# Opening and convolution of an adaLN + S4 + gMLP block: a tick plan replaced by a written list of single steps, phases rounded on TensorE, and K's 32-point product in quarter tiles

## The chip, the core and the metric

One core of a Trainium2 chip. The metric is the device time in microseconds (us) of one execution of the whole program. TensorE appears in the profile as PE (matmuls) and PEld (weight loads), VectorE as DVE, ScalarE as ACT, GpSimd as POOL and SyncE as SP. SP and POOL issue most of the DMAs.

## The reference

The block has two halves with a modulation `mod = silu(c) @ w_mod` in front. The first half is a state-space layer (S4) over 2048 tokens and 576 channels with 128 states each:

```
h  = layernorm(x) * (1 + ca) + sa
K  = real(einsum("dn,dnl,dn->dl", C, exp(dt*A*l), dt*B))     # 576 x 2048
y  = irfft(rfft(h, 4096) * rfft(K, 4096))[:2048] + h * Dskip
x1 = x + ga * y
```

The second half is a gated MLP (`gelu(h2 @ w_in)`, a 2048 x 2048 spatial product, `w_out`) on `x1`. All is float32 at the interface. The change touches only the first half.

## The kernel before

`ssm` (L165) computes the first half. It has two parts, here called opening and convolution.

**Opening.** `poles` (L199) turns the raw S4 parameters into phases and log magnitudes, split in three bf16 parts and stored to DRAM (`pa_d`, `pb_d`); generator `p0` does channel quarter 0, `p1` quarters 1 to 3, at three times the width. `poles_load` (L296) brings them back as `lb`, `lc`, `la`. `mod_unit` (L342) makes six modulation rows. `ln_stats`, `ln_rows` and `ln_half` (L389 to L434) normalise x and do the first forward stage of the transform of h, stored to `u1_d`.

**K, in 36 groups of 16 channels.** `e_unit` (L442): a product into PSUM and `Exp` on ACT. `t_unit` (L456): phases in turns into a PSUM pair `pa`, reduced to the nearest whole turn. For the first `NR = 10` groups TensorE does the rounding by adding and subtracting 12582912 inside the accumulation (L469 beside the L465 products), and DVE copies the rest out (L477). For the other 26 groups ACT adds the constant (L480) and DVE subtracts (L481). L482 takes the absolute value, and `s_unit` (L485) does two `Sin`. `p_unit` (L490): four DVE products. `kg_unit` (L504): 32 products of 128x32 by 128x64 into one bank, copied out by ACT (L514). `d_unit` (L516): a DVE addition of Dskip to 4 columns. `k1_unit` (L520): K's 32-point product, eight float32 products of the 128x64 `kk[:, i]` with a 128x128 block-diagonal matrix that holds the same 32-point block four times, copied out by DVE for odd groups from 11 on (L533), by ACT otherwise (L535).

**Convolution, in 36 units of 512 columns** (five channel blocks of 128, 128, 128, 128 and 64): `u_unit` (L574) a forward product; `z_unit` (L584) K's last stage and the pointwise product on DVE (L591); `v_unit` (L594) the inverse product, stored to `v_d`; `y_unit` (L637), 20 of them, the last stage and the residual addition, stored to `x1_d`. A channel block can be convolved when its eight groups of K are done; it needs `u1_d` of all tokens.

**What sets the order.** The opening, with groups 0 to 8, is a string of units (L725). After it come ticks 9 to 39 (L735): each tick runs one group's units at fixed lags in one of three rotations, and the convolution units by a plan (L656). Then a written tail (L768 to L823) mixes the last units with the preparation of the MLP's first weights. In the ticks the engines' streams are left to the framework; `mlp.tied` marks instructions that keep program order. PSUM tiles: `ps2()` gives one of 2 pairs of banks (`ps`), `ps1()` one of 4 single banks (`pk`). Line 152 (`Pin`) is the recorded line of every tied instruction, so those groups are told apart by their tiles.

After `ssm`, `phase_a` and `phase_b` do the MLP; they are unchanged.

Of the kernel before, what the change touches and what calls it, by code (L numbers as in the profile page):

```python
# [9 lines left out]
F32 = mybir.dt.float32  # L10
# [8 lines left out]
D = 576  # L19
NST = 128  # L20
L = 2048
# [7 lines left out]
GRP = 16  # L29

# [89 lines left out]
def body(tc, I, out):  # L120
    nc = tc.nc
    V, A, G, T, S = nc.vector, nc.scalar, nc.gpsimd, nc.tensor, nc.sync
    with ExitStack() as ctx:
# [6 lines left out]
        V.memset(consts_s[:, 0:1], MAGIC)  # L130
# [34 lines left out]
def ssm(tc, I, x1_d, consts_s, dram, mod_d, mlp):  # L165
    nc = tc.nc
    V, A, G, T, S = nc.vector, nc.scalar, nc.gpsimd, nc.tensor, nc.sync
    magic, halfpi, one = consts_s[:, 0:1], consts_s[:, 1:2], consts_s[:, 2:3]
    HC = 288
    CW = 16 * 9 * 128  # L170
    with ExitStack() as ctx:
# [17 lines left out]
        small = cp.tile([128, 6, 128], F32, name="small")  # L189
        r1 = [small[:, 0], small[:, 1]]  # L190
        fwd, inva, invb, ones = (small[:, i] for i in range(2, 6))
# [7 lines left out]
        def poles(c0, c1, Q, own=None):  # L199
# [8 lines left out]
            def split3(*items):  # L208
# [8 lines left out]
                for src, dst, k, pt, q in parts:  # L217
                    A.activation(pt[:, 0], src, AF.Copy)
                    V.tensor_tensor(q, src, pt[:, 0], op=ALU.subtract)
                    A.activation(pt[:, 1], q, AF.Copy)  # L220
                for src, dst, k, pt, q in parts:
                    V.tensor_tensor(pt[:, 2], q, pt[:, 1], op=ALU.subtract)
                    for c in range(c0, c1):
# [9 lines left out]
            def run():  # L233
# [3 lines left out]
                A.activation(dt, ldt, AF.Exp)  # L237
                V.tensor_tensor(tau, dt, tau, op=ALU.mult)
# [8 lines left out]
                V.tensor_tensor(q1, Ci, Bi, op=ALU.mult)  # L247
                V.tensor_tensor(wr, wr, q1, op=ALU.subtract)
# [7 lines left out]
                V.tensor_tensor(mn, ax, ay, op=ALU.min)  # L256
                V.tensor_scalar(mx, mx, 1e-37, None, op0=ALU.max)
                V.reciprocal(rnd, mx)
                V.tensor_tensor(mn, mn, rnd, op=ALU.mult)
                yield  # L260
                A.activation(lw, mx, AF.Ln)
                AP = mlp.tied.scalar
                AP.activation(q1, mn, AF.Square)
                AP.activation(q1, q1, AF.Ln, bias=one)
                AP.activation(ph, mn, AF.Arctan)
# [4 lines left out]
                split3((al, pb_d, 0), (tau, pa_d, 0))  # L270
                yield
                V.scalar_tensor_tensor(lw, q1, 0.5, lw, op0=ALU.mult, op1=ALU.add)
                V.tensor_tensor(lw, lw, ldt, op=ALU.add)
                split3((tau64, pa_d, 3), (lw, pb_d, 3))
                yield
                V.tensor_scalar(ph, ph, 1.0 / (2 * math.pi), None, op0=ALU.mult)
                V.tensor_tensor(ax, ay, ax, op=ALU.is_gt)
                V.tensor_scalar(ay, ph, -2.0, 0.25, op0=ALU.mult, op1=ALU.add)
                V.tensor_tensor(ay, ay, ax, op=ALU.mult)
                V.tensor_tensor(ph, ph, ay, op=ALU.add)  # L280
                V.tensor_scalar(ay, ph, -2.0, 0.5, op0=ALU.mult, op1=ALU.add)
                V.scalar_tensor_tensor(ay, wr, 0.0, ay, op0=ALU.is_lt, op1=ALU.mult)
                V.tensor_tensor(ph, ph, ay, op=ALU.add)
                yield
                V.scalar_tensor_tensor(ay, wi, 0.0, ph, op0=ALU.is_lt, op1=ALU.mult)
                V.scalar_tensor_tensor(ph, ay, -2.0, ph, op0=ALU.mult, op1=ALU.add)
# [1911 lines left out]
```

## Time and profile before

| | |
|---|---|
| median of 3 runs | 1754.17 us (1753.26 to 1754.69) |
| profiled execution, first to last instruction (span) | 1749.5 us |
| instructions | 36390 |
| busy: PE, PEld, DVE, ACT, POOL | 1654.4, 1241.1, 1256.1, 834.3, 250.5 us |
| first 512-column product of phase A (`pz<-wz,nt`) | 424.2 us |

The span leaves out what lies before the first and after the last instruction; the profiled execution has no separate whole time, so the median less the span, 4.7 us, stands for that. `ssm` fills the first 424 us. In the views "busy" is the union of the instructions' spans. For pipelined matmuls the distance from one start to the next says more than the length of one.

### The profile page before, as it was taken

The page shows a single profiled execution, that of the slowest core. Times are in us where ns is not written, and L with a number is a line of the kernel's source. Part 1 is how long each engine was busy: PE and PEld are TensorE (multiplying, and loading weights), DVE is VectorE, ACT ScalarE, POOL GpSimd, SP SyncE. Part 2 cuts the span into 40 slices and gives each one's busy share as a digit, 9 for nine tenths or more (in the row PEclk, how much of TensorE's full clock was granted, in tenths as well). Part 3 has the DMA queues.
Part 4 walks back from the last instruction along what each step waited for, and adds up shares of the span by engine and source line. Part 5 has one row for each costly group of instructions (what it writes and reads, how often), then busy time and mean ns, then how long its engine had stood idle before and what let it go on. Part 6 is the DMA issues. An engine that isn't in the chain of part 4 may idle for free.

```text
span 1749.5 us, 36390 instructions
## 1 busy us (share of the span) xinstructions
PE 1654.4 (95%) x15174; PEld 1241.1 (71%) x15174; DVE 1256.1 (72%) x2259; ACT 834.3 (48%) x1121; POOL 250.5 (14%) x412
## 2 busy tenths in 40 slices
PE   2788999996999999999999999999999999999999
PEld 1344666664455446777878888888888888888887
DVE  7876999948999997888898767797444387334432
ACT  6877999834677665445443433343221233122210
POOL 4421332342122110000000000000111100111100
PEclk9897999998999999999999999999999999999999
DMA  8477656798698798777656887764766563556531
GB/s 227 136 223 229 187 155 170 207 271 248 215 292 272 222 249 290 258 253 261 221 193 205 289 290 263 241 231 138 246 219 231 195 224 106 194 197 208 193 110 41
DMA packets 182934, 376.24 MB, mean 215 GB/s; under 512 B 39105, under 2 KB 102977, under 8 KB 182001
## 3 DMA queue, kind: packets, MB, share of 16 engines
q1 hardware_dynamic: 138304, 168.50, 31.9%
q0 software_dynamic: 37984, 178.55, 31.2%
q10 hardware_dynamic: 6480, 26.86, 3.8%
q8 instruction: 119, 1.95, 0.5%
q14 instruction: 47, 0.38, 0.1%
HBM read 263.11 MB, written 101.31 MB: 208 GB/s over the span
## 4 chain that ended last, share of the span: by engine, by line
PE 32%; issue 28%; DVE 18%; DMA 4%; POOL 3%; ACT 2%; SPq 0%; POOLq 0%; ACTq 0%; DVEq 0%
PE ps L152 28%; POOL zset L1906 2%; DMA zset<-set_d 2%; DVE bsz L152 2%; DVE zset L152 1%; DVE n L152 1%; DVE gt L152 1%; DVE rq L152 1%; DVE wsp L152 1%; PE pk L578 1%; PE pk L598 1%; PE pk L590 1%; DVE pg L499 1%; DVE wso L152 1%; DVE ft L481 1%
## 5 line engine op out<-in xcount | busy, mean ns | idle before, releaser
L152 PEld LDWEIGHTS <-zset 128*128 128x128 f16 x7182 | 701.9, 98 | 92.6 <-DVE zset L152 7.6
L152 PE MATMUL ps<-wsp,zset 128*128 128x256 f16 x6048 | 667.7, 273 | 7.2 <-DVE zset L152 5.8
L152 PE MATMUL pz<-wz,nt 128*128 128x512 f16 (+1 forms) x1120 | 221.9, 358 | 9.0 <-DVE nt L152 4.3
L152 ACT ACTIVATE z<-gt 128x1024 f16<-128x1024 f32 x56 | 59.0, 1054 | 287.0 <-DVE gt L152 287.0
L152 PEld LDWEIGHTS <-nt 128*128 128x128 f16 x1120 | 109.1, 98 | 115.7 <-DVE nt L152 5.8
L1906 POOL DMA_DIRECT2D zset<-set_d x96 | 50.8, 529 | 869.1 <-PE ps L152 619.7
L152 DVE SCALAR_TENSOR_TENSOR gt<-ps,sc,bsp 128x512 f32<-128x512 f32 x36 | 27.0, 750 | 205.5 <-PE ps L152 203.8
L152 PE MATMUL ps<-wout,z 128*128 128x288 f16 x1344 | 170.0, 286 | 0.0
L152 PEld LDWEIGHTS <-z 128*128 128x128 f16 x1344 | 131.5, 98 | 33.0
L152 PE MATMUL ps<-n2o,zset 128*128 128x256 f16 x1134 | 128.2, 273 | 0.0
L152 DVE SCALAR_TENSOR_TENSOR gt<-ps,sc,gt 128x512 f32<-128x512 f32 (+1 forms) x180 | 122.2, 696 | 7.6
L152 DVE TENSOR_TENSOR raw<-raw 128x512 f32<-128x512 f32 (+2 forms) x228 | 119.2, 528 | 11.2 <-DMA raw<-z_d 6.9
L152 ACT ACTIVATE zset<-raw 128x1792 f16<-128x1792 f32 x48 | 81.2, 1691 | 58.3 <-PE ps L152 25.3
L152 DVE TENSOR_TENSOR zset<-raw,zset 128x1792 f16<-128x1792 f32 x48 | 97.0, 2020 | 15.9 <-ACT zset L152 15.9
L152 DVE TENSOR_TENSOR z<-ps,z 128x512 f32<-128x512 f32 (+1 forms) x126 | 72.0, 599 | 36.8 <-ACT z L152 26.7
L152 ACT ACTIVATE wsp<-raw,sc 128x1792 f16<-128x1792 f32 x25 | 44.6, 1785 | 42.7 <-DVE raw L152 35.0
L152 ACT ACTIVATE z<-z,sc 128x1024 f32<-128x1024 f32 x21 | 24.1, 1148 | 75.6 <-DVE z L152 71.9
L152 ACT ACTIVATE z<-pz,sc 128x512 f32<-128x512 f32 (+1 forms) x96 | 52.0, 582 | 16.2 <-DMA z_d<-z 9.8
L152 PE MATMUL ps<-n2q,wf 128*128 128x512 f16 x252 | 55.7, 379 | 0.0
L152 ACT ACTIVATE z<-z,nm,r 128x1152 f32<-128x1152 f32 x24 | 31.5, 1342 | 49.7 <-DVE nm L152 29.3
L152 PE MATMUL ps<-wout,z1b 128*128 128x288 f16 x384 | 52.6, 286 | 0.5 <-ACT z1b L152 0.5
L152 DVE SCALAR_TENSOR_TENSOR wsp<-raw,sc,wsp 128x1792 f16<-128x1792 f32 x25 | 51.9, 2078 | 0.0
(345 smaller groups left out, 2452.7 us busy)
## 6 DMA issues: line engine op xcount, KB each, us to landing
zset<-set_d POOLq DMA_DIRECT2D x96, 896.0 KB, 4.9
raw<-z_d SPq DMA_DIRECT2D x48, 512.0 KB, 5.5
set_d<-zset ACTq DMA_DIRECT2D x24, 896.0 KB, 5.9
z_d<-z POOLq DMA_DIRECT2D x32, 576.0 KB, 9.7
zset<-wa_d POOLq DMA_DIRECT2D x18, 896.0 KB, 4.9
raw<-in_w_spT SPq DMA_DIRECT2D x25, 512.0 KB, 4.4
set_d<-zset SPq DMA_DIRECT2D x12, 896.0 KB, 5.5
u_d<-st1o POOLq DMA_DIRECT2D x16, 576.0 KB, 4.8
```

What stands on the lines that cost most here:

```text
L152: return self.tc.keep_in_program_order(f(*a, **k))
L481: V.scalar_tensor_tensor(f, f, MAGIC, pa, op0=ALU.subtract, op1=ALU.subtract)
L499: V.tensor_tensor(pr, pi, c3[:, :, None, :].to_broadcast([128, 16, 2, 32]), op=ALU.mult)
L578: T.matmul(pm, fwd, u1, start=True, stop=True)
L590: T.matmul(pm[:, w * j:w * j + w], cst[k // 8][:, k % 8], k1t[c][:, k, :w], start=True, stop=True)
L598: T.matmul(pm, inva, zz[:, 0], start=True, stop=False)
L1906: self.nc.gpsimd.dma_start(o, self.set_d[f, j - 1] if j else self.wa_d[f])
```

## The change

All of opening, K and convolution becomes one list of 1251 steps, `ORDER`. Each unit is a generator that yields between its engines' instructions; a step such as `t9` runs unit t of group 9 up to its next yield. All instructions of `ssm` are tied, so each engine, and each DMA queue, keeps the order of the list. Beside this:

- `t_unit`: all 36 groups are rounded by TensorE (`ROUNDED`); DVE's absolute value and ACT's first `Sin` read PSUM directly; the copy, the ACT addition and the DVE subtraction are gone.
- `k1_unit`: 16 products of 64x64 by 64x64 instead of 8 of 128x64 by 128x128, in a PSUM pair (`ps2`) instead of one bank; ACT alone copies out (`COPIED` is empty).
- `kg_unit`: Dskip is added by four products of a 128x32 slice of an identity with 4 columns; `d_unit` is gone. The identity comes with `small`, now 7 x 128 columns.
- `bs` of the statistics has one buffer instead of two; the branch order in `poles` differs for `p0` and `p1`.

```diff
+ROUNDED = set(range(36))
+COPIED = set()
+ORDER = """
+B2 i2 B0 B7 O0 O0 O0 O0 O0 O0 j1 O0 M2 O0 O0 i1 x0 O0 O0 O0 O0 B6 O0 B4 O0 M1 O0 O0 O0 B1 B3 O0 O0 S0 M2 O0 w3 O0 O0 O0 P0 O0 O0 B5 O0 O0 M2 P0 S1 S0 O0 g1 S0 P0 O0 P0 S1
+S0 P0 P0 S0 Q0 P0 g0 P0 M2 S0 i0 e0 e0 t0 t0 M1 M1 M1 t2 P0 P0 t0 S1 e0 P0 t2 t2 P0 S1 t0 R0 P0 R2 M0 e2 M0 M0 e2 M0 e1 e5 e1 M0 e0 O0 R1 t1 e5 e4 M0 P0 t1 e1 t1 P0 t3 p0
...
+y12 y18 y16 y14 y18 L15 W19 y18 L13 y19 L17 y19 y19 y11
+"""
...
-    nc = tc.nc
+    nc = mlp.tied
...
         def e_unit(g):
...
             for h, (l, r) in enumerate(zip(halves(lb, gi), rows(256, 512))):
                 T.matmul(pa[:, h], l, r, start=True, stop=True)
+            yield
+            e = et[g] = tb.tile([128, 1536], F32, name="et", bufs=5)
             A.activation(e[:, :1024].rearrange("p (h n) -> p h n", h=2), pa, AF.Exp)
+            yield
...
-            if g < NR:
+            if g in ROUNDED:
                 magics(2112, True)
                 phases((768, 0), False, False)
                 magics(2240, False)
                 phases((1536, 1792), False, True)
-                V.tensor_copy(f, pa)
+                yield
+                cs = tt[g] = tb.tile([128, 2, 2, 512], F32, name="ft", bufs=3)
+                ct, f = cs[:, 0], cs[:, 1]
+                V.tensor_single_scalar(ct.bitcast(I32), pa.bitcast(I32), 0x7FFFFFFF, op=ALU.bitwise_and)
+                yield
+                A.activation(f, pa, AF.Sin, scale=-TWO_PI)
             else:
...
+            yield
             A.activation(ct, ct, AF.Sin, bias=halfpi, scale=-TWO_PI)
-            A.activation(f, f, AF.Sin, scale=-TWO_PI)
...
         def kg_unit(g):
             pr, pi, gr, gi = tt.pop(g)
             pm = ps1()
+            for j in range(4):
+                rows = slice(32 * j, 32 * j + 32)
+                T.matmul(pm[rows, 63:256:64], eye[:, rows], dsk[:, 4 * g:4 * g + 4], start=True, stop=False, skip_group_check=True)
...
         def k1_unit(g):
...
-            pm = ps1()
+            pm = ps2()
             for i in range(4):
                 for ri in range(2):
-                    T.matmul(pm[64 * ri:64 * ri + 64, 128 * i:128 * i + 128], kk[:, i], r1[ri], start=True, stop=True,
-                             skip_group_check=True)
...
+                    for h in range(2):
+                        s = slice(64 * h, 64 * h + 64)
+                        T.matmul(pm[64 * ri:64 * ri + 64, h, 64 * i:64 * i + 64], kk[s, i], r1[ri][s, s], start=True, stop=True,
+                                 skip_group_check=True)
+            yield
...
-            if g > 9 and g % 2:
+            if g in COPIED:
...
+        steps = Steps(once, many)
+        for s in ORDER.split():
+            steps.go(s)
...
+    def go(self, s):
+        n, k = s[0], int(s[1:] or 0)
+        if n in self.once:
+            self.once[n](k)
+        else:
+            if s not in self.open:
+                self.open[s] = self.many[n](k)
+            next(self.open[s], None)
```

In the list `O` and `P` are the steps of `p0` and `p1`, `S`, `R`, `A` those of the layer norm and forward stage, `M` of the modulation, `e t p k 1` of the groups, `u z v y` of the convolution, `U W X` its loads, `Q` a `poles_load`, `L` the MLP's preparation, and `B i j g r x w a c f b` loads and single beginnings.

More of the change, by code (lines that the diff above doesn't have):

```diff
@@ L292, in poles @@
+                for part in (second, angle) if own is not None else (angle, second):
+                    yield from part()
+                yield from split3((ph, pa_d, 6))
             return run()
@@ L599, in v_unit, with y_vload @@
             T.matmul(pm, invb, zz[:, 1], start=False, stop=True)
+            yield
+            v = half() if c == NC - 1 and i > 1 else part("v")
             A.activation(v, pm, AF.Copy)
+            yield
             G.dma_start(v_d[c][:, kr(c, i)], by(v, c))
-        def y_vload(c, q):
+        def y_vload(n):
+            c, q = divmod(n, 4)
             bs = slice(4 * q, 4 * q + 4)
@@ new lines, in middle, with st4_load, end, first @@
+        def middle(n):
+            nonlocal cs, sb, wpre
+            early.close()
+            cs, sb, wpre = [ctx.enter_context(tc.tile_pool(name=k, reuse_waits="tile", bufs=b, side="right")) for k, b in (("cs", 1), ("sb", 2), ("wpre", 2))]
+        def st4_load(n):
+            nonlocal st4
+            st4 = cs.tile([128, 16, 2, 64], F32, name="st4")
+            S.dma_start(st4, I["c_st4"])
+        def end(n):
+            tabs.close()
+            mlp.start()
+        def first(n):
+            mlp.ap = mlp.wzp
+            mlp.ln2_stats(0)
+            mlp.roots(x=0)
```

418 lines of the change are left out of this document (177 added, 241 removed), and 3 rows, old and new, of the table T.

## Prediction

> **What bounds the kernel now.** I read the page for the span, then the busy times by stretch up to the start of phase A at 424 us, the timelines of PE inside two of these stretches, the waits of the slack one, and the groups of instructions for durations. The change touches only `ssm`, so the 1325 us behind it stay as they are, and its gain or loss is a shift of the start of phase A.
>
> ```profile
> span 1749.5 us, 36390 instructions
> ```
>
> The six stretches below were cut where the work changes: first pole chain; p1's poles and the first groups; opening with groups 2 to 8; the ticks; the ticks' tail; the transition. Columns: length, then busy time (instructions) of PE, PEld, DVE, ACT, POOL, then the granted clock, DMA share and GB/s.
>
> ```profile
> 0.00:30.00 30.00, 4.06 (x24) 1.55 (x24) 19.46 (x71) 17.31 (x39) 8.96 (x19) 1.00 0.84 224
> 30.00:56.00 26.00, 17.77 (x125) 7.85 (x126) 24.80 (x53) 19.73 (x26) 15.12 (x26) 1.00 0.87 235
> 56.00:153.00 97.00, 76.70 (x1088) 40.25 (x1088) 70.72 (x157) 71.09 (x111) 29.80 (x45) 0.79 0.56 173
> 153.00:341.00 188.00, 179.76 (x2703) 110.69 (x2701) 174.93 (x220) 180.95 (x241) 55.52 (x97) 0.98 0.67 191
> 341.00:395.00 54.00, 53.70 (x526) 36.34 (x523) 27.96 (x41) 21.36 (x32) 20.98 (x35) 1.00 0.92 256
> 395.00:424.00 29.00, 17.39 (x174) 13.40 (x172) 22.86 (x66) 11.72 (x13) 8.04 (x13) 0.76 0.99 295
> ```
>
> From 153 to 341 three engines are over 93% busy; from 341 to 395 PE alone is full while DVE and ACT idle half the time. So from 153 to 395 PE decides: work taken from DVE or ACT there buys little, work added to PE is paid. From 56 to 153 no engine decides: DVE and ACT are busy 71 of 97 us, 73%. Each waits for another in turn:
>
> ```profile
> ACT st1o L433 <- PE ps L431: 11.9, 7, 3.3
> DVE ft L477 <- PE ps L465: 8.7, 4, 4.0
> DVE bs L408 <- DMA ln_x<-in_x: 6.8, 2, 4.2
> DVE rt L420 <- PE ps L431: 4.1, 2, 2.8
> PE ps L448 <- ACT et L449: 2.9, 1, 2.9
> ```
>
> That is a matter of order: 26 us of DVE, 26 of ACT. The change can win here, by its list, and must not lose on PE from 153 on.
>
> **The change part by part.** *PE.* In the ticks an unrounded t_unit takes from 261.07 to 261.31, 0.24 us. A k1_unit takes from 252.80 back to 251.82, 0.98 us; a kg_unit's 64 instructions of 64 columns from 252.80 to 253.71 (the last row starts at 253.60 and holds 0.11 as the others do), 0.91 us, so 14 ns each with four column tiles beside each other.
>
> ```profile
> 251.82 1.04 PE L528 MATMUL pk<-small,kab 128*64 128x128 f32 x16
> 252.80 0.32 PE L511 MATMUL pk<-pg 128*32 128x64 f32 x8
> ...
> 253.60 0.29 PE L511 MATMUL pk<-et,pg 128*32 128x64 f32 x8
> 253.83 1.09 PE L528 MATMUL pk<-small,kab 128*64 128x128 f32 x16
> ...
> 261.07 0.28 PE L465 MATMUL ps<-sel,lc 48*128 48x256 bf16 x2
> 261.19 0.27 PE L465 MATMUL ps<-sel,la 48*128 48x256 bf16 x2
> 261.31 0.39 PE L448 MATMUL ps<-sel,lb 48*128 48x512 bf16 x2
> ```
>
> A rounded t_unit, as the first ten groups have it, takes from 114.48 to 115.36 (the last row below plus 0.11), 0.88 us:
>
> ```profile
> 114.48 0.39 PE L469 MATMUL ps<-sel 48*128 48x512 bf16 x2
> 114.71 0.27 PE L465 MATMUL ps<-sel,lc 48*128 48x256 bf16 x2
> ...
> 115.25 0.27 PE L465 MATMUL ps<-sel,la 48*128 48x256 bf16 x2
> ```
>
> Rounding 26 more groups adds 26 x 0.64 = 16.6 us of PE, all behind 153. For the new k1_unit no row exists: 16 float32 products of 64x64 by 64 columns, 32 instructions. If its four quarters run beside each other as kg's four column tiles do, it costs 32 x 14 ns = 0.46 us; if only two do, twice that, 0.91 us. I take 0.46, because both halves of the argument are in rows: column tiles beside each other in kg, row halves in L465 (two products of 256 columns in 0.11 us). Saved: 0.52 us, and six groups have their k1 ahead of 153 and 30 behind it, so 16 us (2 us at the other bound). Dskip's four products of four columns are 8 instructions more per group; between 8 x 14 ns = 0.11 us and 8 x 61 ns = 0.49 us (k1's 16 in 0.98), I take 0.11, since kg has the same column tiles: 30 x 0.11 = 3.3 us (15 at the other bound). PE from 153 on: +16.6 - 16 + 3.3 = **+4 us** (bounds +4 and +30).
>
> *DVE and ACT.* Columns behind the bar: busy, mean ns; then idle before.
>
> ```profile
> L481 DVE SCALAR_TENSOR_TENSOR ft<-ft,ps 128x1024 f32<-128x1024 f32 x26 | 31.7, 1218 | 2.5 <-ACT ft L480 2.4
> L477 DVE COPY ft<-ps 128x1024 f32<-128x1024 f32 x10 | 12.2, 1221 | 9.8 <-PE ps L465 9.8
> L482 DVE TENSOR_SCALAR ft<-ft 128x1024 int32<-128x1024 int32 x36 | 25.0, 694 | 0.2
> L533 DVE COPY k<-pk 128x512 f32<-128x512 f32 x13 | 8.9, 687 | 1.3 <-PE pk L528 1.2
> L518 DVE TENSOR_TENSOR kab<-kab,dsk 128x4 f32<-128x4 f32 x36 | 5.7, 159 | 3.5 <-ACT kab L514 3.4
> L480 ACT ACTIVATE ft<-ps,consts_s 128x1024 f32<-128x1024 f32 x26 | 29.5, 1133 | 0.0
> L488 ACT ACTIVATE ft<-ft 128x1024 f32<-128x1024 f32 x36 | 38.1, 1057 | 0.0
> L449 ACT ACTIVATE et<-ps 128x1024 f32<-128x1024 f32 x36 | 37.2, 1038 | 1.1 <-PE ps L448 1.0
> L535 ACT ACTIVATE k<-pk 128x512 f32<-128x512 f32 x23 | 13.8, 602 | 1.9 <-PE pk L528 1.8
> L487 ACT ACT_TABLE_LOAD x14 | 18.0, 1283 | 0.2
> ```
>
> DVE loses L481, L477, L533 and L518, 58.5 us. Its absolute value now reads PSUM; bounds are 0.69 us (L482, from SBUF) and 1.22 (L477, the same size from PSUM), I take the latter: +36 x 0.53 = 19. Net -39 us. ACT loses L480, -29.5; takes 13 copies of k1 at 0.60, +7.8; its Sin from PSUM should cost what L449 does, no change. The list also changes the function table more often: counted in the order of its Exp, Ln, Arctan and Sin steps, 43 loads against 34 in the trace before 395; 9 x 1.28 = +11.5. Net -10 us. Behind 153 this relief is worth nothing by itself, PE being the cover; ahead of it it shortens what the list has to pack: 9 groups x (1.22 + 0.69 - 1.22) = 6 us of DVE, while ACT has two of the nine extra loads there.
>
> *The list, 56 to 153.* Its steps up to `C0` hold the same work as before (groups 0 to 8, all of LN, modulation, p1), in finer pieces. With ACT's 71 us at the occupancy of today, 73%, nothing is won; at the 96% of 153 to 341, 71/0.96 = 74 us, 23 are won. I take 85%: 71/0.85 = 84, **-13 us** (bounds 0 and -23; a loss isn't excluded, see the rivals).
>
> *The first chain.* The last store of p0's phases waits 8 us for DVE, and PE's first e_unit comes at 35.41:
>
> ```profile
> 29.67 1.24 POOL L152 DMA_DIRECT2D pa_d<-pt  x2 [8.15 <-DVE pt L152]
> 35.41 1.02 PE L448 MATMUL ps<-sel,lb 48*128 48x512 bf16 x3 [3.09 <-issue]
> 17.41 0.61 DVE L238 TENSOR_TENSOR t_n_A_im<-t_dt,t_n_A_im 128x432 f32<-128x432 f32 x1 [3.69 <-ACT t_dt L237]
> ...
> 28.56 0.60 DVE L242 TENSOR_TENSOR t_n_A_im<-t_n_A_im,t_rnd 128x432 f32<-128x432 f32 x1
> ```
>
> Between these last two rows DVE does 14 operations of p1, ten of 0.52 us start to start and four of 0.29, 6 us in the middle of p0's chain. The list runs all 30 steps of `O` before the fourth of `P`, so **-6 us** (bounds 0 and -8, the wait). p1's work isn't gone: it falls into 30 to 56, where DVE is 95% busy, and spreads to step 252.
>
> *The rest.* POOL and SP issue the same DMAs, now in the list's order. POOL is busy 138 of 424 us, so a late issue there is a matter of what stands ahead of it, not of load. A load on SP that waits for its buffer holds the loads behind it, before as after. The 64 KB more of `small` are hidden by PE's idleness up to 24.9 us of the first weights' load; without that cover they cost 0.3 us at 224 GB/s. The transition from 395 (11.6 us of PE idle) keeps its steps and its DMA round trips: 0.
>
> **Sum.** -6 - 13 + 4 = -15 us: span 1734.5. The median stands 4.7 us above the profiled span (1754.17 - 1749.5), and I carry that over: **1739 us**; this forecast's own range, with the list's occupancy from 78 to 93% (-6 to -21 in place of -13), is 1731 to 1746, and I give it 0.45.
>
> **The rivals.**
>
> *The list packs the ticks and the transition too* (0.2). For it: 8.2 us of PE idle from 153 to 341 and 11.6 from 395 that need not be there, and DVE and ACT now have 26 and 10 us of slack to be early with. Against it: 341 to 395 is already full, and the transition waits for DMA. With the opening at 93% (-21) and the first chain -8: -8 - 21 + 4 - 8 - 6 = -39, 1715 us; at the utmost 1708.
>
> *The quarters don't run side by side* (0.1). Then the change does not do what it says: k1 at 0.91 us and Dskip at 0.49 give PE +30 instead of +4, and the sum is +11: 1765 us; with only the first of the two, +18 and -1: 1753. For it: 64x64 tiles occur nowhere before. Against it: the kg and L465 rows.
> The Trainium skill, "TensorE: Matmul & The Clock Gate", section "Wait — 56ns, not 53.3ns?", says that starts of matmuls are never closer than about 25 ns however few the columns. By that rule alone 32 instructions take an estimated 0.80 us, 30 x 0.18 = 5.4 us are saved in place of 16, and the sum is -4.5: 1750 us. The trace disagrees, kg's 64 instructions have 14 ns, so this outcome has 0.02 of the rival's 0.1.
>
> *PSUM pairs* (0.22, slower). There are two `ps` pairs. An unrounded t_unit holds one for 0.24 + 1.13 + 1.22 = 2.6 us, the new one for 0.88 + 1.22 + 1.06 = 3.2, with DVE and ACT one after the other as the list has them, and k1, which sat in `pk`, takes one for 0.46 + 0.60. With e's 0.4 + 1.04 that is 5.7 us of pair per group in place of 4, and in the opening `ln_half` takes both pairs at once. In a fixed order PE stands still behind a step that has no pair, with kg, u, z, v and y behind it. Price: one wait for the Sin, about 1.0 us, in each of 36 groups, +36, sum +21: 1775 us. It decides from 15/36 = 0.42 us per group on. For it: `PE ps L448 <- ACT et` above. Against it: two pairs offer 14 us in a group's 7 us.
> The Trainium skill, "PSUM — Partial Sum Buffer", section "PSUM bank collisions raise a hardware error", says that two engines may not read one bank at once. By that rule the absolute value and the Sin of one pair cannot overlap, so the 3.2 us could not be 2.1; no run here shows it.
>
> **How the numbers follow.** About 0.2% (3.5 us) is what a measurement of this kernel can tell from no change. Forecast 0.45, all faster. Packed ticks 0.2, faster. Quarters 0.1: half within 0.2%, half slower. Pairs 0.22, slower. The remaining 0.03, a gain that is eaten up to nothing: same. Faster 0.65, same 0.08, slower 0.27. The range reaches to the packed ticks and to the pairs: 1710 to 1776; it leaves out about a third of either, with the bounds of k1 and Dskip inside it.
>
> **What would show it.** Right: the first e_unit on PE near 29 us; the first u_unit (160 us before) near 140; k1's 32 instructions in 0.46 us, t_unit's 12 in 0.88; L480, L481, L477 gone; phase A's first product near 409. Wrong: PE idle behind `ACT ft` or `ACT k` before e, t or k1 for over 0.4 us per group (pairs); k1 over 0.8 us (quarters); ACT and DVE still 73% busy up to the first u_unit (the list's order buys nothing); or SP's loads of u late, with PE waiting for DMA in the ticks.

## The result, and the profile after

The changed kernel takes 1781.25 us (1780.71 to 1784.03), the kernel before 1753.72 beside it: ratio 1.0171, 95% interval 1.0147 to 1.0194. It is slower by 27.5 us between the medians, by 30 by the ratio; 1739 was forecast. The profiled execution took 1781.23 us:

```profile
span 1779.5 us, 38363 instructions
```

The spans differ by 30.0 us. Where they come from is read at three instructions of PE. The timeline of PE in the changed kernel has these rows (start, length, then operation, tiles, shapes and count, idle before and what ended it):

```profile
41.78 0.58 PE L182 MATMUL ps<-sel,lb 48*128 48x512 bf16 x1 [9.70 <-ACT gar L182]
176.41 0.70 PE L182 MATMUL pk<-u,small 128*128 128x512 f32 x1
450.45 0.61 PE L182 MATMUL pz<-wz,nt 128*128 128x512 f16 x1 [0.75 <-ACT nt L182]
```

The same instructions before:

```profile
159.87 0.70 PE L578 MATMUL pk<-u,small 128*128 128x512 f32 x1
424.20 0.61 PE L152 MATMUL pz<-wz,nt 128*128 128x512 f16 x2 [0.69 <-ACT nt L152]
```

| us | first e_unit | first u_unit | first product of phase A | from u to A |
|---|---|---|---|---|
| before | 35.4 | 159.9 | 424.2 | 264.3 |
| after | 41.8 | 176.4 | 450.4 | 274.0 |
| forecast | 29 | 140 | 409 | 269 |

Of the 30 us, 6.4 are lost before the first `e_unit`, 10.1 more up to the first `u_unit`, 9.7 in the ticks and the transition, and 3.8 behind the start of phase A. The last part was not followed.

Busy times by stretch, after (columns as in the prediction), cut at this kernel's own stages:

```profile
0.00:30.00 30.00, 8.75 (x49) 2.57 (x50) 11.34 (x45) 10.03 (x23) 6.76 (x16) 1.00 0.98 283
56.00:82.00 26.00, 16.27 (x162) 7.43 (x166) 18.85 (x32) 20.46 (x28) 7.48 (x12) 0.50 0.15 29
82.00:176.00 94.00, 69.67 (x1315) 37.38 (x1307) 65.12 (x137) 66.68 (x97) 33.68 (x52) 0.71 0.61 190
176.00:363.00 187.00, 176.27 (x3248) 106.74 (x3244) 142.61 (x147) 155.83 (x214) 48.06 (x87) 0.99 0.66 187
363.00:420.00 57.00, 56.81 (x717) 37.45 (x718) 36.83 (x62) 33.42 (x50) 21.35 (x36) 1.00 0.92 252
```

Three things are to be seen. In the first 30 us DVE does 11.34 us of work where it did 19.46, at a DMA share of 0.98. From 82 to 176 DVE and ACT are busy 69 and 71%, no more than before: the list packs nothing. From 176 on PE alone is full (94 and 99.7%), and the relief of DVE and ACT is idle time.

**The first chain.** POOL's timeline starts with loads, and DVE's shows what p0 waits for:

```profile
1.28 1.17 POOL L182 DMA_DIRECT2D wm<-in_w_mod  x2 [0.82 <-POOLq L2174]
2.44 0.56 POOL L182 DMA_DIRECT2D ln_x<-in_x  x1
3.00 1.02 POOL L182 DMA_DIRECT2D k<-in_w_mod  x2
...
17.84 0.31 DVE L182 TENSOR_TENSOR t_wr<-et 128x144 f32<-128x144 f32 x1 [7.08 <-DMA et<-in_A_B_re]
...
34.04 0.30 DVE L182 TENSOR_TENSOR pt<-t_sq,pt 128x144 bf16<-128x144 f32 x1
...
36.64 1.29 POOL L182 DMA_DIRECT2D pa_d<-pt  x2 [0.46 <-DVE t_rnd L182]
37.97 1.05 POOL L182 MEMSET lb<- 32x1152 bf16 x1
39.31 1.03 POOL L182 DMA_DIRECT2D lb<-pb_d  x2 [0.29 <-POOL lb L182]
```

The same steps before (the store of `pa_d`, at 29.67, stands in the prediction):

```profile
4.77 0.31 DVE L152 TENSOR_TENSOR t_wr<-et 128x144 f32<-128x144 f32 x1
...
29.08 0.30 DVE L152 TENSOR_TENSOR pt<-t_sq,pt 128x144 bf16<-128x144 f32 x1
...
32.39 1.03 POOL L152 DMA_DIRECT2D lb<-pb_d  x2 [0.29 <-POOL lb L152]
```

`i2`, `j1` and `i1` of the list, loads of `w_mod` and x, go out first, and p0's own parameters come behind them at a DMA share of 0.98: the product `t_wr` starts 13.1 us later than before. From there to the end of the last part of the phases (`pt`) DVE needs 16.5 us in place of 24.6, 8.1 less. POOL, held to the list, stores that part 2.3 us after it is ready (0.3 before), behind two other loads. From the store to the first `e_unit` it is 5.1 us (5.7 before). Together, 13.1 - 8.1 + 2.0 - 0.6 = 6.4 us.

PE's wait of 9.70 us is put down to the modulation row `gar`, which ends at 41.53. But `lb`, which the product reads, was loaded from 39.31 on and landed some 2.5 us later, at 41.8, when the product starts. So without `gar` PE would have started no sooner.

**PE's new shapes.** Its timeline in the ticks:

```profile
251.96 0.25 PE L182 MATMUL pk<-dsk,small 128*32 128x4 f32 x8
252.04 0.28 PE L182 MATMUL pk<-pg 128*32 128x64 f32 x5
...
261.29 0.69 PE L182 MATMUL ps<-small,kab 64*64 64x64 f32 x32
261.92 0.39 PE L182 MATMUL ps<-sel 48*128 48x512 bf16 x2
...
262.68 0.27 PE L182 MATMUL ps<-sel,la 48*128 48x256 bf16 x2
```

A `k1_unit` takes from 261.29 to 261.92, 0.63 us, 20 ns an instruction. Dskip takes 0.08 us. A rounded `t_unit` takes from 261.92 to 262.68 and 0.11 more, 0.87 us.

**Who holds the pairs.** PE's waits before products into `ps`, after, from 42 to 176 (waiting tile <- what ended the wait: us in total, times, longest):

```profile
PE ps L182 <- ACT st1o L182: 10.8, 12, 1.6
PE ps L182 <- ACT ft L182: 8.4, 6, 2.5
PE ps L182 <- ACT et L182: 2.8, 4, 1.1
```

From 176 to 450 the same view has:

```profile
PE ps L182 <- ACT ft L182: 1.9, 2, 1.3
PE ps L182 <- ACT et L182: 0.8, 1, 0.8
PE ps L182 <- ACT k L182: 0.5, 2, 0.3
```

So PE does wait for pairs, behind the Sin too, but in the opening; in the fitted list's ticks it is 3.2 us, far from one microsecond in each group. Nor is the opening's wait new: before, from 35 to 160 us, the same view has 7.3 us behind the forward stage's copies, 4.0 behind DVE's copy of the phases and 7.9 behind `et`, 19.2 in all where it is 22.0 now.

The groups of instructions from 0 to 450 give the new prices of ACT and DVE:

```profile
L182 ACT ACT_TABLE_LOAD x44 | 56.5, 1283 | 16.4 <-DMA et<-in_A_B_re 14.3 <-PEq L2174 0.7 <-DVE ft L182 0.4
L182 DVE TENSOR_SCALAR ft<-ps 128x1024 int32<-128x1024 int32 x36 | 43.8, 1221 | 27.7 <-PE ps L182 26.8
L182 ACT ACTIVATE ft<-ps 128x1024 f32<-128x1024 f32 x36 | 36.6, 1024 | 27.0 <-DVE ft L182 26.8
```

The absolute value from PSUM takes 1.22 us, the Sin 1.02, and there are 44 table loads: 1.22, about 1.05 and 43 were forecast.

### The profile page after: what moved, and what is told of

It reads as the page before. It is cut to its first block, busy times and chain, and to the rows that moved or that the text cites. A ratio compares the mean times of both kernels' runs of the same rounds, so it can differ in the third digit from the quotient of the medians.

```text
span 1779.5 us, 38363 instructions
## 1 busy us (share of the span) xinstructions
PE 1665.9 (94%) x16246; PEld 1240.0 (70%) x16246; DVE 1233.0 (69%) x2173; ACT 828.9 (47%) x1117; POOL 248.3 (14%) x412
## 4 chain that ended last, share of the span: by engine, by line
PE 67%; DVE 15%; DMA 5%; issue 4%; ACT 2%; POOL 1%; SPq 0%; ACTq 0%; DVEq 0%; POOLq 0%
PE ps L182 58%; PE pk L182 9%; DVE bsz L182 2%; DMA zset<-set_d 2%; DVE n L182 1%; DVE zset L182 1%; DVE rq L182 1%; DVE gt L182 1%; DVE wso L182 1%; DMA uu<-uu 1%; DVE wsp L182 1%; DVE nt L182 1%; DMA wsst<-in_w_spT 1%; DVE bsx L182 1%; DMA z_d<-z 1%
## 5 line engine op out<-in xcount | busy, mean ns | idle before, releaser
L182 ACT ACTIVATE z<-gt 128x1024 f16<-128x1024 f32 x56 | 59.0, 1054 | 282.0 <-DVE gt L182 281.9
L182 DVE TENSOR_TENSOR pg<-et,ft 128x1024 f32<-128x1024 f32 x72 | 85.9, 1218 | 11.9 <-ACT et L182 6.5
L182 DVE TENSOR_TENSOR zz<-pk,uu 128x1024 f32<-128x1024 f32 x36 | 43.9, 1222 | 39.0 <-PE pk L182 31.3
L182 PE MATMUL pk<-zz,small 128*128 128x512 f32 x144 | 69.4, 608 | 0.2 <-DVE zz L182 0.2
L182 ACT ACT_TABLE_LOAD x44 | 56.5, 1283 | 16.4 <-DMA et<-in_A_B_re 14.3
L182 DVE TENSOR_SCALAR ft<-ps 128x1024 int32<-128x1024 int32 x36 | 43.8, 1221 | 27.7 <-PE ps L182 26.8
```

The lines of the kernel that those rows point to most:

```text
L182: return self.tc.keep_in_program_order(f(*a, **k))
```

## The experiments

Ratios are to the kernel before, measured on the same chip beside the run, with 95% intervals; a difference "by the ratios" is theirs times 1754 us. The expectations name their theories by letters or numbers, to which the verdicts refer. "First u" and "u to A" are as in the table above. In the short diffs `ORDER` is cut to its first lines. Four parts: the opening's order, the content without the list, the content inside the list, and a control with before's own order written down.

### The opening's order

`a_dma_later`: the changed kernel, with the loads `i2`, `j1`, `i1` and one modulation product put behind p0's first steps.

```diff
-B2 i2 B0 B7 O0 O0 O0 O0 O0 O0 j1 O0 M2 O0 O0 i1 x0 O0 O0 O0 O0 B6 O0 B4 O0 M1 O0 O0 O0 B1 B3 O0 O0 S0 M2 O0 w3 O0 O0 O0 P0 O0 O0 B5 O0 O0 M2 P0 S1 S0 O0 g1 S0 P0 O0 P0 S1
+B2 B0 B7 O0 O0 O0 O0 O0 O0 O0 O0 O0 x0 O0 O0 O0 O0 B6 O0 B4 O0 i2 j1 M2 O0 O0 O0 B1 B3 O0 O0 S0 M2 O0 w3 O0 O0 O0 P0 O0 O0 B5 O0 O0 M2 P0 S1 S0 O0 g1 S0 P0 O0 P0 S1 S0 P0 P0
...
```

> The changed kernel with only four tokens of its list moved: the loads of w_mod 2 and of the second quarter of x, which POOL issues at 1.3 and 2.4 us ahead of nearly all of the first pole block's parameters, go behind the first store of the phases, w_mod 1 (3.0 us) goes behind the loads of the pole tables, and modulation 1's first product goes behind the first e_unit. Theory A (crowded start): the parameters land some 2 us sooner, the first e_unit comes at 31 to 35 us instead of 41.8, and phase A starts 6 to 10 us sooner: 1771 to 1775 us. Rival (the rest of the opening decides, the list is late anyway): the first e_unit comes sooner, the first u_unit stays near 176 us, 1779 to 1783 us.

Measured: 1791.71 us, 1.0213 (1.0192 to 1.0234). The first `e_unit` comes at 38.1, 3.7 us earlier, but the forward stage starts at 85.8 in place of 82.0, the first u at 183.0. The move wins 3.7 of the 6.4 us and puts another wait in the place of the first: the parameters are on time, and DVE has the phases ready for their last split at 19.6 us, but waits 10.9 us there for ACT, which the list holds behind the copy of a modulation product whose `w_mod` now comes late. The run is 7 us slower by the ratios. Neither theory A's 1771 to 1775 us nor the rival's 1779 to 1783 came, and what the crowded start costs by itself isn't separated.

`a_open_old`: the opening's steps of the list, in the order in which the code before wrote its units.

```diff
...
+B0 B4 O0 O0 O0 O0 O0 O0 O0 O0 B2 g0 O0 O0 O0 O0 O0 O0 O0 g1 B3 B7 x0 i2 O0 O0 O0 O0 O0 O0 O0 O0 O0 O0 O0 O0 O0 O0 O0 M2 M2 M2 M2 B1 B6 B5 Q0 e0 e0 e0 e0 i1 e1 e1 e1 e1 P0 P0
...
```

> The changed kernel with the steps of its list up to C0 put in the order that the kernel before has for its opening (a unit's steps run one after the other again), all edits of the units kept; the steps left over from ahead of C0 follow behind it. Theory B (the order of the opening costs 16 us up to the first u_unit): first u_unit near 160 us, 1762 to 1768 us. Rival (the units' new content costs it, PSUM pairs held longer by t and k1): first u_unit still at 170 or later, 1775 us or more.

Measured: 1855.68, 1.0579 (1.0557 to 1.0601); first u at 248.5. The order before wrote is not the order it ran: its engines' streams were rearranged behind the string of units. Held to it word for word, the opening takes 72 us more than in the change's list. Theory B fell. The rival's range came (first u past 170), but this run doesn't show the pairs to be the cause.

`a_mod_first`: the modulation's `M0` steps in one run, the layer norm's some 40 steps earlier.

```diff
...
-S0 P0 P0 S0 Q0 P0 g0 P0 M2 S0 i0 e0 e0 t0 t0 M1 M1 M1 t2 P0 P0 t0 S1 e0 P0 t2 t2 P0 S1 t0 R0 P0 R2 M0 e2 M0 M0 e2 M0 e1 e5 e1 M0 e0 O0 R1 t1 e5 e4 M0 P0 t1 e1 t1 P0 t3 p0
+P0 P0 S0 Q0 P0 g0 P0 M2 S0 i0 e0 e0 t0 t0 M1 M1 M1 t2 P0 P0 t0 S1 e0 P0 t2 t2 P0 S1 t0 R0 P0 R2 M0 e2 M0 M0 e2 M0 M0 M0 M0 M0 M0 R1 R3 S1 A0 S1 A0 A0 e1 A0 e5 e1 e0 e5 A1 O0
...
```

> The changed kernel with its list reordered in the opening alone: the nine steps of modulation 0 stand together (they are spread over 60 steps), and the layer norm's steps (statistics, rows, ln_half, their loads) stand about 40 steps earlier, where the two PSUM pairs allow it. Theory C (the first ln_half product, 82.0 us against 67.7 before, waits for modulation 0's last rounding at 78.7, and the first u_unit follows the last ln_half by 10 us): first ln_half product at 67 to 72 us, first u_unit at 162 to 168, phase A 8 to 14 us sooner, 1767 to 1773 us. Rival (the opening is set by the sum of its waits, not by where ln_half starts): last ln_half product still near 167 us, 1779 to 1784 us or more.

Measured: 1795.09, 1.0233 (1.0207 to 1.0258). The forward stage now starts at 67.5, as early as before, but ends at 171.7, and the first u is at 194.5. A late start of that stage isn't what costs the opening; theory C fell too, and the rival's range came. Three changes by hand each made the list worse.

### The content without the list

These put parts of the change into the kernel before, whose engines' streams stay free. `b_content` has all of it but the list; `b_quarter` the quarters of `k1_unit` alone (in a pair); `b_t_psum` the absolute value and the Sin straight from PSUM, for the ten groups that were rounded before too.

```diff
# b_quarter
-            pm = ps1()
+            pm = ps2()
...
-                    T.matmul(pm[64 * ri:64 * ri + 64, 128 * i:128 * i + 128], kk[:, i], r1[ri], start=True, stop=True,
+                    for h in range(2):
...
# b_t_psum
-                V.tensor_copy(f, pa)
+                V.tensor_single_scalar(ct.bitcast(I32), pa.bitcast(I32), 0x7FFFFFFF, op=ALU.bitwise_and)
+                A.activation(f, pa, AF.Sin, scale=-TWO_PI)
```

> The kernel before with its own orders and its free engines, and only the content of the units changed: all 36 groups rounded by TensorE with the absolute value and the first Sin read from PSUM, K's product in quarters, Dskip by TensorE. Theory (the list costs the opening, content costs only PE in the ticks: +16.2 for t, +2.4 for Dskip, -10.8 for k1): 1759 to 1764 us. Rival 1 (content is the whole loss, by the two PSUM pairs): 1772 us or more. Rival 2 (relief of VectorE and ScalarE pays): 1750 us or less.

> The kernel before with K's 32-point product in quarters alone (and Dskip's host layout to match). Theory (PE decides from 153 us on, a k1_unit costs 0.63 us in place of 0.98): 30 x 0.35 = 10.5 us less, 1742 to 1746 us. Rival 1 (ScalarE, 96% busy, and VectorE, 93%, take over as soon as PE is relieved): 1749 to 1753 us. Rival 2 (k1 in a ps pair makes e and t wait): 1755 us or more.

> The kernel before with t_unit's new second half for its ten rounded groups alone: absolute value and Sin read the PSUM pair, no copy, so that VectorE has 10 x 0.69 = 7 us less and a pair is held for 1.0 us more. Theory D (pairs): the opening becomes longer, first u_unit at 162 or later, 1756 to 1764 us. Rival (VectorE's relief wins): first u_unit at 154 to 159, 1748 to 1753 us.

| | median | ratio | first u | u to A |
|---|---|---|---|---|
| b_content | 1788.76 | 1.0195 (1.0175 to 1.0216) | 174.5 | 282.0 |
| b_quarter | 1765.44 | 1.0062 (1.0043 to 1.0081) | 164.1 | 267.4 |
| b_t_psum | 1768.99 | 1.0082 (1.0056 to 1.0107) | 165.4 | 269.8 |

The content alone loses 34 us by the ratio without any list, as rival 1 had it; that the pairs are the reason is not shown by it. `b_t_psum` has the late first u of its theory D, but lies above its range of 1756 to 1764; its waits of PE behind the Sin are 4.6 us, all in the opening. `b_quarter` takes work off PE and adds none. The stretch from 190 to 310 us before:

```profile
190.00:310.00 120.00, 117.46 (x1793) 73.48 (x1782) 117.11 (x149) 116.15 (x156) 37.94 (x66) 1.00 0.57 158
```

and in `b_quarter`:

```profile
190.00:310.00 120.00, 109.00 (x1979) 65.26 (x1977) 115.59 (x147) 114.11 (x154) 39.90 (x70) 1.00 0.55 158
```

PE has 8.5 us less to do, and the stage is no shorter. Before, three engines were at the limit there, not PE alone: DVE and ACT were 98 and 97% busy, and in `b_quarter` they are still 96 and 95%. But PE also has a new wait in this stretch. Its rows before `ps` come to 9.3 us, where before has none; the largest two are

```profile
PE ps L530 <- DVE k L535: 3.5, 3, 1.4
PE ps L530 <- ACT k L537: 3.2, 3, 1.3
```

So the relief is eaten up by waits for a pair that a nearly full DVE or ACT frees late, and this run doesn't tell the pair from the full engines. The theory (1742 to 1746) and rival 1 (1749 to 1753) fell; rival 2's range, 1755 or more, came.

### The content inside the list

Three parts undone in the changed kernel, its list kept. `a_k1_whole`: `k1_unit` as before, in one bank. `a_t_copy`: DVE copies the phases out, absolute value and Sin read SBUF. `a_round10`: only the first ten groups rounded by TensorE; in the others ACT's addition and DVE's two operations stand in one step.

```diff
# a_k1_whole
-            pm = ps2()
+            pm = ps1()
...
# a_t_copy
-                V.tensor_single_scalar(ct.bitcast(I32), pa.bitcast(I32), 0x7FFFFFFF, op=ALU.bitwise_and)
+                V.tensor_copy(f, pa)
+                V.tensor_single_scalar(ct.bitcast(I32), f.bitcast(I32), 0x7FFFFFFF, op=ALU.bitwise_and)
...
# a_round10
-ROUNDED = set(range(36))
+ROUNDED = set(range(10))
...
```

> The changed kernel with K's product as before: eight full products of 64 columns into a pk buffer in place of quarters in a ps pair. Theory A2 (TensorE decides in the stretch from the first u_unit on, pairs matter little): 30 x 0.37 = 11 us more, 1790 to 1794 us. Rival (the pair that k1 takes makes e and t wait, in the opening above all, as the kernel before with quarters alone suggests by its 11 us): 1776 to 1784 us.

> The changed kernel with one edit in t_unit: VectorE copies the phases out of PSUM as before (1.22 us) and takes the absolute value from SBUF (0.69 us), ScalarE's Sin reads SBUF. The PSUM pair is free after 0.9 + 1.2 us, not 3.2; VectorE has 36 x 0.69 = 25 us more, 9 x 0.69 = 6 us of it in the opening. Theory D (pairs held through the Sin cost the opening): last ln_half product and first u_unit 3 to 8 us sooner, 1773 to 1778 us. Rival (the pair is not what is waited for): the opening pays VectorE's 6 us, the rest is covered by TensorE, 1781 to 1788 us.

> The changed kernel, its list kept, with only the first ten groups rounded by TensorE, the others as before (ScalarE copy, two VectorE operations, the pair free after 2.6 us, the Sin from SBUF): TensorE 16.6 us less, ScalarE 30 us more, VectorE 50 - 32 = 18 us more, behind the first u_unit for the most part. Theory J (in the fitted list TensorE decides from 176 us on): 1766 to 1776 us. Rival G (ScalarE, 33 of 40 us busy there, and the chain through it become the bound): 1782 us or more.

| | median | ratio | first u | u to A |
|---|---|---|---|---|
| a_k1_whole | 1797.37 | 1.0241 (1.0217 to 1.0265) | 176.5 | 290.9 |
| a_t_copy | 1801.01 | 1.0259 (1.0234 to 1.0285) | 184.1 | 282.9 |
| a_round10 | 1816.33 | 1.0367 (1.0339 to 1.0395) | 179.3 | 315.9 |

By the ratios they lose 12, 15 and 34 us against the changed kernel. `a_k1_whole` loses about what theory A2 had for it, 11 us of PE's work, though its median lies above the range of 1790 to 1794: from its first u to phase A PE is busy 265.5 us, 14.1 more than in the changed kernel, and waits for no pair. `a_round10` loses though it takes 16 us from PE (theory J fell, rival G's range came); `a_t_copy` pays for 25 us of DVE work (36 times 0.69) that has idle time beside it (theory D fell, and it lies above the rival's 1781 to 1788 too). The stretch of `a_round10` from 176 to 363:

```profile
176.00:363.00 187.00, 152.45 (x2437) 87.07 (x2429) 135.78 (x145) 151.09 (x200) 41.55 (x76) 0.90 0.56 160
```

No engine is over 82%: the three wait for one another in an order that was made for other durations. Undoing a part inside a fitted list can measure the fit and not the part. So `a_t_copy` and `a_round10` don't say what a part is worth; `a_k1_whole`, in the same shape of list, does agree with PE's price for the quarters.

### A control: before's own order, written down

`o_all_old` has the list's machinery, and the content of before. Its list was sorted by the times at which before's trace ran each step (p1's steps stand behind p0's). Nothing is fitted to the new content, and the order is before's as far as whole steps allow.

```diff
-B2 i2 B0 B7 O0 O0 O0 O0 O0 O0 j1 O0 M2 O0 O0 i1 x0 O0 O0 O0 O0 B6 O0 B4 O0 M1 O0 O0 O0 B1 B3 O0 O0 S0 M2 O0 w3 O0 O0 O0 P0 O0 O0 B5 O0 O0 M2 P0 S1 S0 O0 g1 S0 P0 O0 P0 S1
+B0 g0 O0 O0 B4 O0 B2 B3 O0 x0 B1 O0 O0 O0 B7 O0 O0 O0 O0 O0 O0 O0 O0 O0 O0 O0 B6 g1 B5 i2 O0 S0 O0 S0 O0 O0 S0 O0 S0 O0 M2 S0 O0 O0 O0 O0 w3 O0 M2 O0 P0 P0 P0 P0 P0 P0 M2 P0
...
-ROUNDED = set(range(36))
+ROUNDED = {0, 1, 2, 3, 4, 5, 6, 7, 8, 9}
```

> Control: the changed kernel's machinery, a written list of single steps with every engine held to it, but with the content of before's units and with the list sorted by the times at which before's trace shows each step starting (the second pole block's steps stand behind the first block's, and a group of operations that the list knows as one step stays one). Theory E (the order in which the work stands is what decides): the time of before within 1%, 1750 to 1770 us, first u_unit at 155 to 168. Rival (holding the engines to single steps costs by itself): first u_unit at 172 or later, 1775 us or more.

Measured: 1789.73, 1.0186 (1.0169 to 1.0203); first u at 192.4, u to A 263.5. Theory E fell, the rival's range came. In the ticks, holding the engines to a written order costs nothing (264.3 before). In the opening it costs 32.5 us, though the first `e_unit` comes at 33.2, earlier than before's 35.4. The busy times of before up to its first u:

```profile
0.00:160.00 160.00, 104.41 (x1345) 53.27 (x1346) 118.75 (x285) 115.10 (x183) 54.18 (x89) 0.87 0.68 197
```

and of the control up to its own:

```profile
0.00:192.00 192.00, 100.80 (x1340) 51.16 (x1341) 126.26 (x284) 116.75 (x182) 54.21 (x89) 0.82 0.57 164
```

It is the same work, some 1340 products and 182 operations on ACT, in 32 us more. Before's streams had been arranged instruction by instruction; a step holds several of them together. One place can be seen, ACT's and PE's rows of the control:

```profile
39.59 0.56 ACT L182 ACTIVATE t_lw<-t_n_B_re 128x432 f32<-128x432 f32 x1 [6.05 <-DVE t_n_B_re L182]
...
49.76 1.02 ACT L182 ACTIVATE et<-ps 128x1024 f32<-128x1024 f32 x1
50.83 0.61 PE L182 MATMUL ps<-sel 48*128 48x512 bf16 x2 [13.45 <-ACT et L182]
```

Before, the first of these rows stands at 31.30 and the first `Exp` at 40.53. In the control p1's steps stand behind p0's, so p1's logarithm (`t_lw`) comes 8.3 us later, ACT is held to it, and the first `Exp` comes 9.2 us later; PE waits 13.45 us for its pair. So a part of the 32.5 us is p1's place and not the form of the list. What the remainder hangs on stays open.

On this control the parts can be weighed one at a time. `a_order_old` puts all of the new content into its order. `o_quarter` has the quarters in a pair, `o_quarter_pk` the same quarters in two single banks. `o_t36` rounds all 36 groups and reads PSUM directly, `o_t36_copy` rounds all 36 and lets DVE copy them out. `o_dsk` has Dskip on PE. Steps that would wait for a buffer that a later step frees had to be moved: 44, 21, 5, 19, 0 and 0 of them.

```diff
# o_quarter
-            pm = ps1()
+            pm = ps2()
# o_quarter_pk
-            pm = ps1()
+            pms = [ps1(), ps1()]
...
# o_t36
-COPY_OUT = {0, 1, 2, 3, 4, 5, 6, 7, 8, 9}
+COPY_OUT = set()
# o_dsk
+            for j in range(4):
+                rows = slice(32 * j, 32 * j + 32)
+                T.matmul(pm[rows, 63:256:64], eye[:, rows], dsk[:, 4 * g:4 * g + 4], start=True, stop=False, skip_group_check=True)
```

> All of the changed content (36 rounded groups read from PSUM, quarters, Dskip by TensorE), in a list sorted by the times of before's trace; a step stands earlier than there only where a PSUM pair has to be free first (44 places). Theory E (the written list's own order is what loses, content costs about the 9 us of TensorE): 1760 to 1770 us. Rival F (the content costs in any order, because a pair is held through VectorE and ScalarE and k1 needs one too; the written list had been fitted to that): 1780 us or more, longer than the changed kernel.

> The control with K's product in quarters alone, in the same list but for 21 places where a PSUM pair has to be free first. TensorE's k1 falls from 1.0 to 0.63 us in each group. Theory E: 4 to 10 us less than the control. Rival F (k1 takes a pair from e and t): the time of the control or up to 10 us more.

> The control with the new t_unit alone for all 36 groups (19 places moved for the pairs): TensorE +16.6 us from group 10 on, VectorE -56 +19 us, ScalarE -30 us. Theory E (TensorE decides from 160 us on): 8 to 17 us more than the control, all of it behind the first u_unit. Rival F: 20 us or more, a good part of it ahead of the first u_unit. Rival G (VectorE and ScalarE decide): less than the control.

> As o_quarter, but a k1_unit takes two of the four pk buffers in place of one of the two ps pairs and copies each half by itself (36 more copies, about 0.2 us each on ScalarE or VectorE); 5 places moved instead of 21. Theory F (the pair that k1 takes from e and t is what costs o_quarter its 21 us over the control): 1778 to 1793 us, at most 3 above the control's 1789.7, and TensorE's waits for ps back near the control's 65 us. Rival H (any change of the units' shape in an order made for others costs this): 1803 us or more.

> The control with all 36 groups rounded by TensorE as in o_t36 (16.6 us more of TensorE from group 10 on), but with VectorE copying the phases out as before does for its first ten groups, so that a pair is held for 0.9 + 1.2 us instead of 3.2; VectorE's work is that of the control, ScalarE's 30 us less. Theory F (what costs o_t36 its 28 us is the pair held through the Sin): 1795 to 1807 us, the difference to the control being TensorE's. Rival I (TensorE's longer t_unit is what costs): 1814 to 1822 us.

> The control with Dskip added by TensorE in place of VectorE: TensorE +2.4 us, VectorE -5.7 us, one wait of VectorE for kab less in each group, no PSUM pair. Theory F (only pairs cost): 1785 to 1793 us. Rival H (any change costs): 1797 us or more.

| | median | ratio | over the control | first u | u to A |
|---|---|---|---|---|---|
| o_all_old | 1789.73 | 1.0186 (1.0169 to 1.0203) | | 192.4 | 263.5 |
| a_order_old | 1847.06 | 1.0510 (1.0488 to 1.0531) | +57 us | 201.6 | 308.3 |
| o_quarter | 1810.42 | 1.0309 (1.0291 to 1.0326) | +22 | 198.9 | 282.1 |
| o_quarter_pk | 1786.90 | 1.0191 (1.0168 to 1.0215) | +1 | 187.3 | 268.3 |
| o_t36 | 1818.26 | 1.0359 (1.0344 to 1.0374) | +30 | 204.7 | 283.8 |
| o_t36_copy | 1798.51 | 1.0251 (1.0221 to 1.0281) | +11 | 195.6 | 276.6 |
| o_dsk | 1785.09 | 1.0184 (1.0161 to 1.0207) | 0 | 191.6 | 265.9 |

("Over the control" is by the ratios.) `a_order_old` and `o_t36` came in rival F's ranges; `o_quarter` came its way, but twice as far as its 10 us. `o_quarter_pk`, `o_t36_copy` and `o_dsk` came in theory F's ranges. The same quarters cost 22 us in a pair and nothing that can be measured in two single banks. PE's waits before `ps` in the ticks of `o_quarter`, 199 to 481:

```profile
PE ps L182 <- ACT et L182: 17.8, 11, 2.8
PE ps L182 <- DVE ft L182: 5.1, 3, 3.0
PE ps L182 <- DVE k L182: 1.2, 1, 1.2
```

of the control, 192 to 456:

```profile
PE ps L182 <- DVE ft L182: 1.8, 1, 1.8
PE ps L182 <- ACT et L182: 0.5, 1, 0.5
```

and of `o_quarter_pk`, 187 to 456:

```profile
PE ps L182 <- ACT et L182: 1.3, 2, 1.0
```

The wait isn't behind `k` itself: with a third user, e and t come to a pair sooner than it is free, and PE stands behind them.

For the phases the same holds of the Sin. `o_t36` in its ticks, 205 to 488:

```profile
PE ps L181 <- ACT ft L181: 9.7, 10, 2.3
PE ps L181 <- ACT et L181: 2.2, 3, 0.8
```

and `o_t36_copy`, 196 to 472:

```profile
PE ps L182 <- DVE ft L182: 2.8, 1, 2.8
```

`o_t36_copy` has as much PE work as `o_t36` and more DVE work, and is faster by 1.08% of 1754 us, 19 us: that is the pair held through the Sin, net of the copies. Nearly half of it lies ahead of the first u, which comes at 195.6 in place of 204.7. The other 11 us go with rounding on PE. So in this order the pairs cost about 22 + 19 = 41 us, the steps moved for them included, and Dskip nothing. That a pair is held so long can be seen in the changed kernel's own timeline of DVE and ACT:

```profile
72.72 1.22 DVE L182 TENSOR_SCALAR ft<-ps 128x1024 int32<-128x1024 int32 x1
73.97 1.02 ACT L182 ACTIVATE ft<-ps 128x1024 f32<-128x1024 f32 x1 [4.05 <-DVE ft L182]
```

The Sin needs nothing that the absolute value makes; yet it starts 0.03 us behind its end. So do 18 of the 36, within 0.04 us; the others start later, and none before its absolute value is done (26.8 us of ACT's idle time are put down to `DVE ft`). Both write halves of one tile `ft`, but that doesn't hold them apart: before, DVE reads one half (L499) from 139.80 us while ACT writes the other (L488) from 140.31. What they share besides is the pair. This is what the Trainium skill says in "PSUM — Partial Sum Buffer", section "PSUM bank collisions raise a hardware error": two engines may not read one bank at once. The trace agrees, with no overlap in 36 cases.

### A version without pairs

`b_quarter_pk`: the kernel before with the quarters in two single banks. `b_quarter_pk_dsk`: that and Dskip on PE. In the control's order these two parts had cost nothing that can be measured.

```diff
-            pm = ps1()
+            pms = [ps1(), ps1()]
...
```

> The kernel before, its engines free, with K's product in quarters that go to two pk buffers instead of a ps pair (b_quarter with the pair given back; each half copied by itself). Theory F (the pair cost b_quarter its 11 us): 1745 to 1757 us. Rival H (before stands at the best of its own order, any new shape costs some 10 us): 1762 us or more.

> The same with Dskip by TensorE as well: the two parts of the change that take no ps pair. Theory F: 1742 to 1755 us, a version that may be faster than before. Rival H: 1762 us or more.

Measured: 1765.86, 1.0083 (1.0062 to 1.0105), and 1767.98, 1.0090 (1.0067 to 1.0112). Their first u comes at 161.1 and 160.8, and u to A takes 277.8 and 278.8, so the loss is in the ticks. Neither beats the kernel before: theory F fell, rival H's range came. With free streams the loss doesn't hang on the pair: in a pair the quarters had 1.0062. No version found is faster than the kernel before.

## Why the prediction was wrong, step by step

- **First chain, -6: it came to +6.4.** The step weighed the order of `O` and `P` only. What it forecast did come: p0's chain on DVE is 8.1 us shorter, with p1's work no longer in its middle. But a term that was put at nothing ate it up: the parameters are 13.1 us late behind the list's early loads through POOL, and POOL stores the phases 2.0 us later. These loads were in the list to be read. The prediction wrote "a late issue there is a matter of what stands ahead of it" and did not look.
- **Opening, -13: it came to +10.1.** The step took the low occupancy, 73%, for a bad order that a written one would mend. ACT and DVE are at 71 and 69% afterwards, as the prediction named for this failing. The control shows that a written order of whole steps loses 32.5 us there even with before's work and, p1's place apart, before's own times.
- **PE behind the first u, +4: it came to 8.3.** 26 groups of rounding at 0.63 us are 16.4; the quarters save 30 x 0.35 = 10.5, not 16; Dskip adds 2.4. The mis-sized term is the quarter: 20 ns an instruction, between the two values weighed (14 and 28). The Trainium skill, "TensorE: Matmul & The Clock Gate", section "Wait — 56ns, not 53.3ns?", has about 25 ns as the least; the trace, with 20, contradicts it here. By busy time PE has 251.4 us of work from 176 to 450 where it had 245.0 from 160 to 424, 6.4 more, and 3.6 more idle. So most of the stretch's 9.7 us is PE's own work.
- **"From 153 to 395 PE decides": half right.** In the changed kernel it does, as `a_k1_whole` bears out. Before, DVE and ACT were at the limit with it from 190 to 310, and PE's relief there gained nothing in `b_quarter`, where waits for a pair have their part in it.
- **Behind 153 the relief of DVE and ACT is worth nothing: right.** They are at 76 and 83% from 176 to 363, and the stage is no shorter. The prices of the absolute value, the Sin, the copies (0.60) and the table loads were right too.
- **Rivals.** "Packed ticks" did not come: they are longer. "Quarters not side by side" came in part, as above. "PSUM pairs" gave 1775 us and slower, close to the time measured, and the mechanism exists; but the changed kernel isn't that case as it was worked out, and the nearness of the number is chance. Its one microsecond in each of 36 groups was paid in the control's order (41 us), where nothing was fitted to it. In the fitted list it is 3.2 us in the ticks, and in the opening 8.4 behind the Sin and 10.8 behind the forward stage's copies, where before had 4.0 behind DVE's copy and 7.3. The argument against it, that two pairs offer 14 us in a group's 7, fell: an average says nothing of when a pair is free in a fixed order.

By the ratios, the sum in place of -6 - 13 + 4 is: +33 us for the control's order, whole steps with p1 behind p0, +57 for the new content in that order (22 and 30 for quarters and phases alone, 0 for Dskip, the rest not separated), and -60 from there to the change's own list (1.0510 to 1.0171): +30. That list makes up for two thirds of what its form and the content cost. The 4.7 us that the prediction carried from the span to the median are no part of one execution: the changed kernel's profiled execution, 1781.23 us, is 1.7 above its span.

Open: which whole steps, beside p1's place, cost the control's opening, and how the 10.1 us of the changed kernel's divide between them and the pairs; why the kernel with free streams loses 11 to 16 us by any new shape in it (`b_quarter`, `b_quarter_pk`, `b_t_psum`, `b_quarter_pk_dsk`), where a rearranged stream is likely and was not shown; and the 3.8 us behind phase A.

## What to carry to other kernels

A stage without a full engine isn't thereby badly ordered: before pricing a written order as a gain, write down the present one and time it. A buffer is priced by how long each user holds it, in the order in which an engine comes to it, not by its mean offer; in the control's order a third user of two buffers cost 22 us that two other buffers made vanish. A part that is taken out of a list fitted to it can measure the fit. Beside it belongs a run that changes the same shape but not the buffer in question, as `o_quarter_pk` does beside `o_quarter`.

## What the runs showed of the hardware

- Float32 products of 64x64 tiles by 64 columns ran at 20 ns an instruction (32 in 0.63 us), and 128x32 by 4 columns at 10 ns (8 in 0.08 us).
- The granted clock of PE was 0.50 from 56 to 82 and 0.71 from 82 to 176 us in the changed kernel, in stretches where PE is busy 63 and 74%; before had 0.79 from 56 to 153 at 79%. The busy share alone doesn't set it: `a_dma_later` had 1.00 from 56 to 82 at 62%.
- Nor does the clock explain the opening's loss. `a_dma_later`, with 1.00 and 0.81 in the two stretches, has its first u later still, and four executions of the changed kernel with mean granted clocks of 0.969, 0.977, 0.986 and 0.983 took 1781.23, 1781.27, 1780.71 and 1784.03 us.
